# Banded attention followed by a leaky-ReLU MLP: an opening with sums ahead of products, the first hidden tiles of a half advanced pair by pair over four banks, and other gates for the loads of batches 1 and 2

## The chip, the core and the metric

The kernel runs on one core of one Trainium2 chip. The metric is the device time of one execution in microseconds, as the median over runs. The engines are named as in the profile: PE is TensorE's matmuls and PEld its weight loads, DVE is VectorE, ACT ScalarE, POOL GpSimd, SP SyncE (which here only issues DMAs). The letter q behind a name (SPq, ACTq) means the engine's instruction queue rather than its arithmetic.

## What is computed

Eight batches of eight heads attend over 576 tokens within a window of 32 to each side. The result, as 4608 tokens by 512 channels, goes through two matrices with a leaky ReLU between them.

```python
# q, k, v: (8, 8, 576, 64); w_in: (512, 2048); w_out: (2048, 512); all float32
scores = np.matmul(q, k.transpose(0, 1, 3, 2)) / np.sqrt(64)
mask = np.abs(pos[:, None] - pos[None, :]) <= 32
attn = softmax(np.where(mask, scores, -1e9))
x = np.matmul(attn, v).transpose(0, 2, 1, 3).reshape(4608, 512)
h = x @ w_in
out = np.maximum(0.01 * h, h) @ w_out
```

## The kernel before

**Units of work.** Two heads, p and p+4, share the 128 partitions and are called a pair. A half is 288 of a batch's 576 tokens. One attention step i is one pair of one half of one batch: `where(i)` (L233) gives batch i//8, half (i//4)%2 and pair i%4, so there are 64 steps. A half g of the MLP needs the four steps of that half, because `xT` (the attention output, transposed) holds one pair in each of its four 128-channel chunks.

**One batch on its way to a step.** SP loads q, k (`load_qk`, L64, two DMAs a pair) and v (`load_v`, L77, two DMAs a pair). `cast_qk` (L166) casts q and k to bf16, q on DVE or POOL and k on POOL. `transposes` (L190) turns them on PE into a bank of PSUM, ACT copies them to `qT` and `kT` (L208, L214), and `place_keys` (L220) lets DVE put the keys into the block-diagonal `kbd` (L226). `cast_v` (L172) puts v into the block-diagonal `vbd`. Both block-diagonal tiles must have been set to zero first, `clear` (L118) on ACT or a memset.

**One step.** `score` (L236) is five matmuls into `ps`, an exponential on ACT (`e`, L247) and the product with the band's mask on POOL (`pr`, L251). `weighted` (L267) multiplies `pr` by a block of ones for the row sums `s` (L275 and L278, or L273 after `join` has added the two parts of `pr`), then `pr` by v for `x` (five matmuls, L285); DVE takes the reciprocal `r` of `s` (L291) and multiplies `x` by it into `xT` (L293). `s` and `x` have one PSUM bank each (`xps`, L58), so the next `s` waits for this reciprocal and the next `x` for this multiplication.

**The MLP.** `h_tile(g, f)` (L299) is four accumulating matmuls, one for each pair's chunk c of `xT` (L304), and a leaky ReLU on ACT into `gT` (L308). There are 16 such tiles in a half. `o_tile(j)` (L312) is sixteen accumulating matmuls for 128 tokens (L321), a copy on ACT (L326) and a store that ACT issues (L327). Hidden tiles, output tiles and transposes rotate over the four banks of `mmps` (L56).

**The order.** `manual_schedule` (L45) keeps every engine in the order of the program text, so an instruction that waits holds back all that is behind it on its engine. Every DMA of SP and ACT takes the next of eight semaphores in turn, and its issue waits until the DMA that had that semaphore before it has landed, whichever queue issued that one. The opening (L424 to L485) is written out by hand: batch 0 is cast and transposed, steps 0 to 3 run one after another with `keep_busy` (L329: matmuls whose result nobody reads) between them, the weights are loaded by POOL (`load_w_in`, eight DMAs, L409; `load_w_out`, four, L415) between POOL's other work; then the 16 hidden tiles of half 0 with steps 4 to 7 between them, then batch 1's transposes between the 16 tiles of half 1, and scores 8 and 9. From L490 on a plan of matmul times sets for every step a due time, and `spend` (L512) calls `step` (L360) when the plan's clock passes it.

**Gates on the loads.** `load_qk(..., behind)` first copies one element of a given tile into the place that the load will fill (L70; `load_v`: L81). As the copy must follow the writer of that element, and the load must follow the copy, the load and all that SP issues later wait. Before, batch 1's q and k wait in this way for `w_in`'s second chunk of columns (L456), and batch 1's v for `w_out`'s second chunk (L470). Batch 2's q and k are issued with no gate, ahead of steps 8 to 11 (L521), and its v after steps 10 to 13 (L524).

Of the kernel before, what the change touches and what calls it, by code (L numbers as in the profile page):

```python
# [16 lines left out]
def kernel(  # L17
# [34 lines left out]
    prob = ctx.enter_context(tc.tile_pool(name="prob", bufs=4))  # L52
# [73 lines left out]
    clear(vbd[0], 1)  # L126

# [10 lines left out]
    for lo in (0, 64):  # L138
        w = win[lo:lo + 64]
        nc.gpsimd.affine_select(  # L140
            out=w, in_=w, compare_op=ALU.is_ge, fill=0.0,
            base=0, channel_multiplier=-1, pattern=[[0, 3], [1, 128]],
        )
        nc.gpsimd.affine_select(
            out=w, in_=w, compare_op=ALU.is_ge, fill=0.0,
            base=2 * W, channel_multiplier=1, pattern=[[0, 3], [-1, 128]],
        )
    win_f = win.rearrange("p n c -> p (n c)")
# [87 lines left out]
    def score(i):  # L236
        b, hf, p = where(i)
        ps = scps.tile([128, 1024], FP32, name="ps")
        c0 = 512 - HALF
        for blk, q0, n in WIN[hf]:  # L240
            nc.tensor.matmul(  # L241
                ps[:, c0:c0 + n], kbd[b % 2][:, p, blk],
                qT[b][:, p, q0:q0 + n], start=True, stop=True,
            )
            c0 += n
        e = attn.tile([128, NCOL], BF16, name="e")
        nc.scalar.activation(  # L247
            out=e, in_=ps[:, 512 - HALF:512 - HALF + NCOL], func=AF.Exp, scale=scale,
        )
        pr = prob.tile([128, NCOL], BF16, name="pr")  # L250
        nc.gpsimd.tensor_mul(pr, e, mask[hf])  # L251
        probs[i] = pr, None

    def join(i):
# [4 lines left out]
        both = prob.tile([128, HALF], BF16, name="both")  # L259
# [5 lines left out]
        probs[i] = pr, both  # L265

    def weighted(i):  # L267
        b, hf, p = where(i)
        pr, both = probs.pop(i)
        x = xps.tile([128, HALF], FP32, name="x")  # L270
# [3 lines left out]
        else:  # L274
# [6 lines left out]
            )  # L281
        c0 = 0
# [7 lines left out]
        r = attn.tile([128, HALF], FP32, name="r")  # L290
        nc.vector.reciprocal(r, s)  # L291
        t0 = (b * S + hf * HALF) % RING
        nc.vector.tensor_mul(xT[:, p, t0:t0 + HALF], x, r)  # L293
# [4 lines left out]

    def h_tile(g, f):  # L299

        t0 = g * HALF % RING
        h = mmps.tile([128, 512], FP32, name="mm", tag="mm")
        for c in range(DMC):
            nc.tensor.matmul(  # L304
                h[:, 0:HALF], w_in_bf[:, c, ts(f, 128)], xT[:, c, ds(t0, HALF)],
                start=(c == 0), stop=(c == DMC - 1),
            )
        nc.scalar.activation(  # L308
            out=gT[:, f, ds(t0, HALF)], in_=h[:, 0:HALF], func=AF.Prelu, alpha=0.01,
        )  # L310
# [49 lines left out]
    def step():  # L360
# [10 lines left out]
        if i < 7:  # L371
            score(i + 1)
        elif 8 <= i < NC - 2:
            nb, _, np_ = where(i + 2)
            if nb >= BY_DMA:
                step_transposes(8 * nb + 2 * np_ + 2)
                place_keys()
            score(i + 2)
# [28 lines left out]
    def load_w_in(f0, f1):  # L407
        for a in range(2):
# [20 lines left out]
    clear(vbd[0], 2)  # L429
    cast_v(0, 0)  # L430
    cast_qk(0, 2, nc.vector)
    score(0)
    load_w_in(0, 512)
    first_pair()
    clear(vbd[0], 3)
    cast_qk(0, 3, nc.vector)
    load_w_in(512, 1024)
    for i in range(NPAIR):
        score(i + 1)
        if i + 1 < NPAIR:  # L440
            cast_v(0, i + 1, on_act=True)
        if i < 2:
            load_w_in(1024 + 512 * i, 1536 + 512 * i)
        else:
            load_w_out(i - 2)
        if i > 0:
            keep_busy(3 if i == 1 else 2)
        weighted(i)
        if i == 0:
            first_pair()  # L450
    state["done"] = NPAIR

    for p in range(NPAIR):
        load_qk(1, p, w_in_bf[0:1, 0, 512:514] if p == 0 else None)  # L456
    keep_busy(2)
    step()
    load_w_out(2)
    load_w_out(3)  # L460
    for f in range(FFC):
        h_tile(0, f)
        if f in (2, 6, 10):
            step()
        if f % 4 == 3:
            nc.gpsimd.memset(kbd[1][:, f // 4], 0.0)
    cast_qk(1, 0, nc.vector)
    cast_qk(1, 1, nc.vector)
    for p in range(NPAIR):
        load_v(1, p, w_out_bf[0:1, 4, 0:2] if p == 0 else None)  # L470
    second = transposes(1)
    for f in range(FFC):
        h_tile(1, f)
        if f % 4 == 3:
            p = f // 4
            next(second)
            next(second)
            place_keys()
            if p + 2 < NPAIR:
                cast_qk(1, p + 2, nc.vector)  # L480
            nc.gpsimd.memset(vbd[1][:, p], 0.0)
        if f == 11:
            score(8)
    state["tp"] = 16
    score(9)  # L485
# [18 lines left out]
    due = []  # L504
    for i in range(8, NC):
        prev = 0.9 * O_US * 4 if i < 12 else at[i // 4 - 1] - LEAD
        due.append(prev + (at[i // 4] - LEAD + (1.2 if i < 12 else 0) - prev) * (i % 4 + 1) / 4)
# [4 lines left out]
    def spend(us):  # L512
        nonlocal clock, turn
        while due and due[0] <= clock:
            due.pop(0)
            i = state["done"]
            if i < 11:
                cast_v(1, i - 7)

            if i < 12:  # L520
                load_qk(2, i - 8)  # L521
            step()
            if 10 <= i < 14:
                load_v(2, i - 10)  # L524
# [42 lines left out]
```

## Time and profile before

| What | Value |
|---|---|
| three runs | 331.64 us median, 330.44 to 332.67 |
| profiled execution | 330.4 us, of which the profiled span is 328.7 us |
| busy share of the span | PE 94%, DVE 70%, ACT 66%, PEld 63%, POOL 55% |
| `h` matmuls, 128x288 (L304) | 1024, 286 ns each in the profile; sixteen in a row take 1.96 us |
| `o` matmuls, 128x512 (L321) | 592; sixteen in a row take 3.45 us |
| reciprocal (L291) | 64, 1954 ns each |
| multiplication into `xT` (L293) | 64, 458 ns each |
| loads | q and k 288 KB each, v 144 KB in each of two DMAs, `w_in` 256 KB and `w_out` 512 KB each as stored |

The span of 328.7 us lies inside the 330.4 us of the execution, so 1.7 us lie around it. A line of the timeline gives start, duration, engine, line of the program, operation, out<-in, number of instructions merged, and in brackets the idle time before it with what ended it. A line of the waits gives who waited for whom, the total in us, how often, and the longest. A matmul's own duration contains its passage through the array; what a row of matmuls costs is its end less its start.

### The profile page before, as it was taken

The page shows a single profiled execution, that of the slowest core. Times are in us where ns is not written, and L with a number is a line of the kernel's source. Part 1 is how long each engine was busy: PE and PEld are TensorE (multiplying, and loading weights), DVE is VectorE, ACT ScalarE, POOL GpSimd, SP SyncE. Part 2 cuts the span into 40 slices and gives each one's busy share as a digit, 9 for nine tenths or more (in the row PEclk, how much of TensorE's full clock was granted, in tenths as well). Part 3 has the DMA queues.
Part 4 walks back from the last instruction along what each step waited for, and adds up shares of the span by engine and source line. Part 5 has one row for each costly group of instructions (what it writes and reads, how often), then busy time and mean ns, then how long its engine had stood idle before and what let it go on. Part 6 is the DMA issues. An engine that isn't in the chain of part 4 may idle for free.

```text
span 328.7 us, 6685 instructions
## 1 busy us (share of the span) xinstructions
PE 308.3 (94%) x2533; PEld 207.3 (63%) x2533; DVE 228.5 (70%) x310; ACT 218.5 (66%) x432; POOL 180.3 (55%) x213
## 2 busy tenths in 40 slices
PE   2578999699999999999999999999999999999996
PEld 1446784367675676758485666767675767666653
DVE  4489744588795987879786988789768867565200
ACT  6775791358493674878988887878786655554541
POOL 7698747667783695519751497339642545221000
PEclk9999999999999999999999999999999999999999
DMA  8999979969995489935997199947831001010102
GB/s 181 215 199 220 269 179 208 235 164 231 200 212 162 152 146 208 226 106 125 194 232 146 64 160 226 194 127 94 173 90 65 34 3 63 2 64 3 64 8 89
DMA packets 80309, 47.11 MB, mean 143 GB/s; under 512 B 59156, under 2 KB 75796, under 8 KB 80276
## 3 DMA queue, kind: packets, MB, share of 16 engines
q1 hardware_dynamic: 70660, 33.04, 52.9%
q10 hardware_dynamic: 5328, 9.44, 8.4%
q0 software_dynamic: 4288, 4.20, 7.6%
q8 instruction: 20, 0.33, 0.4%
q14 instruction: 13, 0.11, 0.1%
HBM read 36.70 MB, written 9.44 MB: 140 GB/s over the span
## 4 chain that ended last, share of the span: by engine, by line
PE 79%; DMA 6%; DVE 6%; SPq 3%; ACT 3%; issue 1%; POOL 1%; ACTq 0%; DVEq 0%
PE mm L304 36%; PE mm L321 31%; DVE r L291 4%; PE x L285 4%; PE ps L241 4%; DMA kf<-in_k_dram 2%; DMA out_dram<-o_sb 2%; PE s L273 2%; SPq L83 2%; PE tp L200 2%; DMA vf<-in_v_dram 2%; ACT kT L214 1%; SPq L72 1%; DVE xT L293 1%; ACT qT L208 1%
## 5 line engine op out<-in xcount | busy, mean ns | idle before, releaser
L291 DVE RECIPROCAL r<-s 128x288 f32<-128x288 f32 x64 | 125.1, 1954 | 38.0 <-PE s L273 28.4
L251 POOL TENSOR_TENSOR pr<-e,mask 128x544 bf16<-128x544 bf16 x64 | 77.8, 1216 | 103.9 <-ACT e L247 82.1
L304 PE MATMUL mm<-xT,w_in_bf 128*128 128x288 bf16 x1024 | 133.5, 286 | 0.4 <-DVE xT L293 0.4
L321 PE MATMUL mm<-w_out_bf,gT 128*128 128x512 bf16 (+2 forms) x592 | 130.1, 373 | 0.0
L308 ACT ACTIVATE gT<-mm 128x288 bf16<-128x288 f32 x256 | 100.8, 415 | 20.6 <-PE mm L304 8.1
L304 PEld LDWEIGHTS <-w_in_bf 128*128 128x128 bf16 x1024 | 98.2, 98 | 24.7 <-issue 0.8
L321 PEld LDWEIGHTS <-gT 128*128 128x128 bf16 x592 | 56.4, 98 | 59.8
L247 ACT ACTIVATE e<-ps 128x544 bf16<-128x544 f32 x64 | 40.0, 624 | 26.2 <-DMA vf<-in_v_dram 4.8
L326 ACT ACTIVATE o_sb<-mm 128x512 f32<-128x512 f32 (+2 forms) x37 | 21.6, 585 | 53.7 <-PE mm L321 53.7
L226 DVE COPY kbd<-kT 64x576 bf16<-64x576 bf16 x64 | 28.5, 446 | 25.6 <-ACT kT L214 24.9
L178 POOL CAST vbd<-vf 64x576 bf16<-64x576 f32 x58 | 38.8, 669 | 2.0
L293 DVE TENSOR_TENSOR xT<-x,r 128x288 bf16<-128x288 f32 x64 | 29.3, 458 | 6.7
L168 POOL CAST kb<-kf 96x768 bf16<-96x768 f32 x32 | 27.5, 858 | 10.0 <-DMA kf<-in_k_dram 10.0
L241 PE MATMUL ps<-qT,kbd 128*128 128x128 bf16 (+2 forms) x320 | 26.8, 216 | 2.8 <-ACT e L247 2.8
L241 PEld LDWEIGHTS <-kbd 128*128 128x128 bf16 x320 | 20.8, 101 | 11.0 <-issue 3.3
L285 PE MATMUL x<-pr,vbd 128*128 128x128 bf16 (+2 forms) x320 | 26.3, 214 | 1.5 <-DVE xT L293 1.0
L262 DVE TENSOR_TENSOR both<-pr 128x256 bf16<-128x256 bf16 x52 | 23.4, 449 | 3.5 <-POOL pr L251 2.4
L285 PEld LDWEIGHTS <-vbd 128*128 128x128 bf16 x320 | 20.9, 99 | 5.0 <-issue 1.9
L264 DVE COPY both<-pr 128x32 bf16<-128x32 bf16 x52 | 23.8, 459 | 0.0
L168 POOL CAST qb<-qf 96x768 bf16<-96x768 f32 x24 | 19.7, 820 | 0.0
L208 ACT ACTIVATE qT<-qT 128x576 bf16<-128x576 bf16 x16 | 18.8, 1176 | 0.9 <-ACT o_sb L326 0.8
L214 ACT ACTIVATE kT<-kT 128x576 bf16<-128x576 bf16 x16 | 18.8, 1176 | 0.0
(39 smaller groups left out, 121.4 us busy)
## 6 DMA issues: line engine op xcount, KB each, us to landing
qf<-in_q_dram SPq DMA_DIRECT2D x32, 288.0 KB, 5.1
kf<-in_k_dram SPq DMA_DIRECT2D x32, 288.0 KB, 5.4
vf<-in_v_dram SPq DMA_DIRECT2D x64, 144.0 KB, 5.1
out_dram<-o_sb ACTq DMA_DIRECT2D x35, 256.0 KB, 2.5
w_in_bf<-in_moe_w_in_dram POOLq DMA_DIRECT2D x8, 256.0 KB, 6.7
w_out_bf<-in_moe_w_out_dram POOLq DMA_DIRECT2D x4, 512.0 KB, 13.0
qT<-qb SPq DMA_TRANSPOSE x16, 4.4
kT<-kb SPq DMA_TRANSPOSE x16, 4.2
```

The lines of the kernel that those rows point to most:

```text
L168: eng.tensor_copy(out=dst[:, p], in_=src[b, p].rearrange("p a (c d) -> p c a d", d=D),)
L178: nc.gpsimd.tensor_copy(out=vbd[b % 2][r, p, :, r], in_=vf[b, p][r])
L226: nc.vector.tensor_copy(out=kbd[b % 2][r, p, :, r], in_=kT[r].rearrange("p (n j) -> p n j", j=64),)
L241: nc.tensor.matmul(ps[:, c0:c0 + n], kbd[b % 2][:, p, blk], qT[b][:, p, q0:q0 + n], start=True, stop=True,)
L247: nc.scalar.activation(out=e, in_=ps[:, 512 - HALF:512 - HALF + NCOL], func=AF.Exp, scale=scale,)
L251: nc.gpsimd.tensor_mul(pr, e, mask[hf])
L285: nc.tensor.matmul(x[:, a:a + n], vbd[b % 2][:, p, blk, :], pr[:, c0:c0 + n], start=(n_ == 0), stop=(n_ == len(WIN[hf]) - 1), skip_group_c ...
L291: nc.vector.reciprocal(r, s)
L293: nc.vector.tensor_mul(xT[:, p, t0:t0 + HALF], x, r)
L304: nc.tensor.matmul(h[:, 0:HALF], w_in_bf[:, c, ts(f, 128)], xT[:, c, ds(t0, HALF)], start=(c == 0), stop=(c == DMC - 1),)
L308: nc.scalar.activation(out=gT[:, f, ds(t0, HALF)], in_=h[:, 0:HALF], func=AF.Prelu, alpha=0.01,)
L321: nc.tensor.matmul(o[:, lo:hi], gT[:, f, ds(128 * j % RING, 128)], w_out_bf[:, f, lo:hi], start=(f == 0), stop=(f == FFC - 1),)
```

## The change

- `weighted` is cut into `sums` (the sums' matmuls and the reciprocal), `product` (the five matmuls with v) and `scaled` (the multiplication into `xT`). Reciprocals get a pool of three buffers, `pr` six in place of four, the joined `pr` a pool of its own.
- The opening is written anew. Scores 0 and 1 come ahead of the third transposes, `sums(0)` between the two transposes of pair 2. All nine matmuls of `keep_busy` go. `w_in`'s first chunk is loaded in two parts, head group 0 after the second product with the mask and head group 1 after the third; the other `w_in` chunks follow, and `w_out`'s after the products with the mask of scores 4 and 5. ACT clears `vbd[0]` for pairs 0 to 2 at the start, POOL for pair 3.
- `h_first` computes the first four hidden tiles of a half chunk by chunk: the four matmuls for c = 0, one in each of four banks, then those for c = 1, and so on. In half 0, the products, sums and scores of pairs 2 and 3 stand ahead of c = 2 and c = 3.
- Batch 1's q, k and v are loaded in one run behind one gate, `w_out`'s first chunk. Batch 2's loads stand behind the steps: each pair behind its own step's `xT`.
- Batch 1's first two casts of q on DVE (`cast_qk(1, 0)`, `cast_qk(1, 1)`) stand ahead of the last step of half 1 (`second_half()` for i = 7), and `h_first(1)` follows that step. The transposes of batch 1's pair 0 come after tile 13 of half 1, those of pairs 1 to 3 and scores 8 and 9 among the output tiles, and steps 8 to 11 at fixed due times.

The order in which DVE has the instructions around that last step, as the changed program is compiled (its own line numbers: L287 the reciprocal, L172 the casts, L313 the multiplication, L230 the keys):

```
L287 Reciprocal r<-s
L172 TensorCopy qb<-qf   (batch 1, pair 0)
L172 TensorCopy qb<-qf   (batch 1, pair 1)
L313 TensorTensor xT<-x,r
L230 TensorCopy kbd<-kT
```

```diff
+    def sums(i):
         b, hf, p = where(i)
-        pr, both = probs.pop(i)
-        x = xps.tile([128, HALF], FP32, name="x")
+        pr, both, _ = probs[i]
         s = xps.tile([128, HALF], FP32, name="s")
         if both is not None:
             nc.tensor.matmul(s, ones_bd, both, start=True, stop=True)
...
+        r = recip.tile([128, HALF], FP32, name="r")
+        nc.vector.reciprocal(r, s)
+        probs[i][2] = r
+
+    def product(i):
+
+        b, hf, p = where(i)
+        pr = probs[i][0]
+        x = xps.tile([128, HALF], FP32, name="x")
         c0 = 0
         for n_, (blk, q0, n) in enumerate(WIN[hf]):
...
-        r = attn.tile([128, HALF], FP32, name="r")
-        nc.vector.reciprocal(r, s)
+        probs[i][1] = x
+
+    def place(i):
+
+        b, hf, p = where(i)
         t0 = (b * S + hf * HALF) % RING
-        nc.vector.tensor_mul(xT[:, p, t0:t0 + HALF], x, r)
+        return xT[:, p, t0:t0 + HALF]
+
+    def scaled(i):
+        _, x, r = probs.pop(i)
+        nc.vector.tensor_mul(place(i), x, r)
+
+    def weighted(i):
+        if probs[i][2] is None:
+            sums(i)
+        product(i)
+        scaled(i)
...
+    def h_first(g, hooks):
+
+        hs = [mmps.tile([128, 512], FP32, name="mm", tag="mm") for _ in range(4)]
         for c in range(DMC):
-            nc.tensor.matmul(
-                h[:, 0:HALF], w_in_bf[:, c, ts(f, 128)], xT[:, c, ds(t0, HALF)],
-                start=(c == 0), stop=(c == DMC - 1),
-            )
-        nc.scalar.activation(
-            out=gT[:, f, ds(t0, HALF)], in_=h[:, 0:HALF], func=AF.Prelu, alpha=0.01,
-        )
+            if c in hooks:
+                hooks[c]()
+            for f in range(4):
+                h_mms(g, f, hs[f], (c,))
+        for f in range(4):
+            h_out(g, f, hs[f])
...
-        if i < 7:
-            score(i + 1)
-        elif 8 <= i < NC - 2:
+        if 8 <= i < NC - 2:
...
-    def load_w_in(f0, f1):
-        for a in range(2):
+    def load_w_in(f0, f1, heads=(0, 1)):
+        for a in heads:
...
     cast_qk(0, 1, nc.vector)
     first_pair()
     first_pair()
-    clear(vbd[0], 2)
     cast_v(0, 0)
+    score(0)
     cast_qk(0, 2, nc.vector)
-    score(0)
-    load_w_in(0, 512)
-    first_pair()
-    clear(vbd[0], 3)
+    score(1)
+    load_w_in(0, 512, (0,))
+    next(first)
+    sums(0)
+    next(first)
+    product(0)
+    place_keys()
     cast_qk(0, 3, nc.vector)
+    scaled(0)
+    sums(1)
+    cast_v(0, 1, on_act=True)
+    score(2)
+    load_w_in(0, 512, (1,))
     load_w_in(512, 1024)
-    for i in range(NPAIR):
-        score(i + 1)
-        if i + 1 < NPAIR:
-            cast_v(0, i + 1, on_act=True)
-        if i < 2:
-            load_w_in(1024 + 512 * i, 1536 + 512 * i)
-        else:
-            load_w_out(i - 2)
-        if i > 0:
-            keep_busy(3 if i == 1 else 2)
+    next(first)
+    next(first)
+    place_keys()
+    product(1)
+    scaled(1)
+    cast_v(0, 2, on_act=True)
+    load_w_in(1024, 1536)
+    sums(2)
+    score(3)
+    load_w_in(1536, 2048)
+
+    def before_2():
+        product(2)
+        scaled(2)
+        cast_v(0, 3, on_act=True)
+        sums(3)
+        score(4)
+        load_w_out(0)
+
+    def before_3():
+        product(3)
+        scaled(3)
+        sums(4)
+        score(5)
+        load_w_out(1)
+
+    state["done"] = NPAIR
+
+    def second_half():
+
+        i = state["done"]
         weighted(i)
-        if i == 0:
-            first_pair()
-    state["done"] = NPAIR
-
-
-
-    for p in range(NPAIR):
-        load_qk(1, p, w_in_bf[0:1, 0, 512:514] if p == 0 else None)
-    keep_busy(2)
-    step()
+        if i < 7:
+            sums(i + 1)
+        if i < 6:
+            score(i + 2)
+        state["done"] += 1
+
+    h_first(0, {2: before_2, 3: before_3})
     load_w_out(2)
     load_w_out(3)
-    for f in range(FFC):
+
+    for p in range(NPAIR):
+        load_qk(1, p, w_out_bf[0:1, 0, 0:2] if p == 0 else None)
+    for p in range(NPAIR):
+        load_v(1, p)
+    second_half()
+    for f in range(4, FFC):
         h_tile(0, f)
-        if f in (2, 6, 10):
-            step()
-        if f % 4 == 3:
-            nc.gpsimd.memset(kbd[1][:, f // 4], 0.0)
+        if f in (7, 11):
+            second_half()
+        if f % 2 == 1:
+            nc.gpsimd.memset((kbd if f < 12 else vbd)[1][:, (f - 4) // 2 % 4], 0.0)
     cast_qk(1, 0, nc.vector)
     cast_qk(1, 1, nc.vector)
-    for p in range(NPAIR):
-        load_v(1, p, w_out_bf[0:1, 4, 0:2] if p == 0 else None)
     second = transposes(1)
-    for f in range(FFC):
+
+    def second_pair(p):
+        next(second)
+        next(second)
+        place_keys()
+        if p + 2 < NPAIR:
+            cast_qk(1, p + 2, nc.vector)
+
+    second_half()
+    h_first(1, {})
+    for f in range(4, FFC):
         h_tile(1, f)
-        if f % 4 == 3:
-            p = f // 4
-            next(second)
-            next(second)
-            place_keys()
-            if p + 2 < NPAIR:
-                cast_qk(1, p + 2, nc.vector)
-            nc.gpsimd.memset(vbd[1][:, p], 0.0)
-        if f == 11:
-            score(8)
+        if f == 13:
+            second_pair(0)
+        if f in (7, 9):
+            nc.gpsimd.memset(vbd[1][:, (f - 3) // 2], 0.0)
     state["tp"] = 16
-    score(9)
 
 
 
@@ -501,27 +574,35 @@
         if kind == "h" and f == 0:
             at[g] = t
         t += us
-    due = []
-    for i in range(8, NC):
-        prev = 0.9 * O_US * 4 if i < 12 else at[i // 4 - 1] - LEAD
-        due.append(prev + (at[i // 4] - LEAD + (1.2 if i < 12 else 0) - prev) * (i % 4 + 1) / 4)
+    due = [
+        (0.0, lambda: score(8)), (1.0, lambda: second_pair(1)), (2.6, lambda: second_pair(2)),
+        (3.2, lambda: score(9)), (4.4, lambda: second_pair(3)),
+    ]
+    due += [(6.0 + 1.9 * n, step) for n in range(NPAIR)]
+    for i in range(12, NC):
+        prev = at[i // 4 - 1] - LEAD if i >= 16 else 11.9
+        due.append((prev + (at[i // 4] - LEAD - prev) * (i % 4 + 1) / 4, step))
     clock = 0.0
     cast_v(1, 0)
     turn = 0
 
     def spend(us):
         nonlocal clock, turn
-        while due and due[0] <= clock:
-            due.pop(0)
+        while due and due[0][0] <= clock:
+            what = due.pop(0)[1]
+            if what is not step:
+                what()
+                continue
             i = state["done"]
             if i < 11:
                 cast_v(1, i - 7)
-
+            step()
+
+            mark = place(i)[0:1, 0:2]
             if i < 12:
-                load_qk(2, i - 8)
-            step()
+                load_qk(2, i - 8, mark)
             if 10 <= i < 14:
-                load_v(2, i - 10)
+                load_v(2, i - 10, mark)
 
```

## The prediction

> **What bounds the kernel now.** I read the page's slices first, then each engine's timeline for the first 70 us, then the waits. TensorE is busy nearly everywhere; its slices fall below 9 only in the first four and in the eighth (57.5 to 65.7 us). The DMA engines are full for the first 60 us.
>
> ```profile
> PE 308.3 (94%) x2533; PEld 207.3 (63%) x2533; DVE 228.5 (70%) x310; ACT 218.5 (66%) x432; POOL 180.3 (55%) x213
> ...
> PE   2578999699999999999999999999999999999996
> ...
> DMA  8999979969995489935997199947831001010102
> ```
>
> So a change of the opening is worth what it does to TensorE's time up to 70 us; from there both versions have the same work. Four rows of TensorE's timeline: from x of step 4 at 27.49 it runs without a gap through the 32 hidden tiles, and the first output matmul starts at 48.46.
>
> ```profile
> 27.49 0.40 PE L285 MATMUL x<-pr,vbd 128*128 128x64 bf16 x5 [0.15 <-DVE xT L293]
> 27.73 1.63 PE L304 MATMUL mm<-xT,w_in_bf 128*128 128x288 bf16 x12
> ...
> 48.46 5.34 PE L321 MATMUL mm<-w_out_bf,gT 128*128 128x512 bf16 x24
> ...
> 62.99 0.40 PE L241 MATMUL ps<-qT,kbd 128*128 128x64 bf16 x5 [2.16 <-ACT e L247]
> ```
>
> After that its rows show idle times of 0.34, 0.61, 2.16, 0.15 and 0.23, in all 3.5 us up to 70. The two longest end with `e` on ScalarE, which itself stood behind a store's issue that waited for batch 1's and batch 2's loads:
>
> ```profile
> PE ps L241 <- ACT e L247: 2.8, 2, 2.2
> ...
> ACT e L247 <- DMA vf<-in_v_dram: 4.8, 1, 4.8
> ...
> ACT e L247 <- DMA kf<-in_k_dram: 3.6, 1, 3.6
> ```
>
> VectorE's rows: the last step of half 1 is finished before batch 1's first casts, which wait for loads.
>
> ```profile
> 35.28 1.96 DVE L291 RECIPROCAL r<-s 128x288 f32<-128x288 f32 x1
> 37.34 0.46 DVE L293 TENSOR_TENSOR xT<-x,r 128x288 bf16<-128x288 f32 x1
> 37.71 1.49 DVE L168 CAST qb<-qf 96x768 bf16<-96x768 f32 x2
> ```
>
> SyncE's rows: a gate is issued when its writer has landed, and the loads behind it start when the gate's copy has landed: 4.5 us after its start the first time, 8.7 us the second.
>
> ```profile
> 22.95 0.73 SPq L70 DMA_DIRECT2D qf<-w_in_bf  x1
> ...
> 27.48 0.33 SPq L72 DMA_DIRECT2D qf<-in_q_dram  x1
> ...
> 28.39 0.40 SPq L72 DMA_DIRECT2D qf<-in_q_dram  x1
> ...
> 37.73 0.62 SPq L81 DMA_DIRECT2D vf<-w_out_bf  x1
> ...
> 46.42 6.38 SPq L83 DMA_DIRECT2D vf<-in_v_dram  x8
> ```
>
> **The opening up to half 1.** Score 0's `e` loses the clear ahead of it and starts at about 10.2 (11.22 before). From there by durations of the rows: `pr` 0 ends 12.1, sums 0 at 12.9 (low clock), reciprocal 0 at 14.9, pair 2's keys (0.91) 15.8, score 2 16.5, `e` 17.2, `pr` 2 18.4. Only then is the second part of `w_in`'s first chunk issued (14.78 before). The first q load, on an empty queue, landed in 3.4 us; the fastest of the eight `w_in` loads, all queued, in 5.9. So it lands between 21.8 and 24.3; batch 0's last load landed at 19.9, the queue is idle, so I take 22.2. The c = 0 and c = 1 matmuls wait for it ahead of x 2: eight at 0.24 (low clock) end 24.2, x 2 and its multiplication end 25.3 (24.98 before), reciprocal 3 and multiplication 3 end 27.7 (27.44 before). Sums ahead of products gained 2 us earlier, and the wait for `w_in` takes them back. Next, sums 5 wait for reciprocal 4 (28.2 to 30.15). From 30.2 TensorE has until c = 3 of half 1: twelve tiles (5.88), twelve matmuls (1.47) and eight small groups of 0.24: it gets there at 39.5, and reciprocal 7 ends about 38.2. The nine `keep_busy` matmuls lay in TensorE's waits for VectorE; taking them out saves nothing, and they count for the clock below.
>
> **The step that decides: multiplication 7.** In the changed order both batch-1 casts stand on VectorE between reciprocal 7 and multiplication 7. Behind it waits c = 3 of the first four hidden tiles of half 1, and behind those all of TensorE. The casts need the second q load, third in the run of batch 1, whose gate has moved from `w_in`'s second chunk to `w_out`'s first.
> - `w_out`'s first chunk landed at 32.9 (issued 24.07, 8.9 later) at the end of a stream without a hole: `w_in`'s eight loads land 1.32 apart. The later second load can open a hole of 0 to 2.6 us. I take 33.0.
> - The gate's copy: 4.5 or 8.7 by the rows above, 3.0 (a v load at 46.42 on idle engines) at the least. 8.7 was behind eight loads of its own queue, which is empty here, while `w_out`'s chunks 2 to 4 are moving as `w_in` was in the first case: 4.5, so 37.5.
> - First q issue to second q landed: 9.7 before (27.48 to 28.39 + 8.8) with `w_out` beside it all the time; 5.7 for batch 0 alone (0.81 to 1.74 + 4.8). A `w_out` chunk alone takes 2.6 (twice 1.32), so chunks 2 to 4 end at about 40.9: half the bandwidth is gone for 2.6 of the time. 5.7 + 1.3 = 7.0, so 44.5 (bounds 41.6 and 53.9).
> - Cast 0.56, multiplication 0.46, 0.15 to TensorE: c = 3 starts at 45.7, an idle time of 6.2 us where there was none.
>
> **What follows.** From c = 3 TensorE has 13 tiles less what is done (6.4), eight groups of transposes (2.04) and scores 8 and 9 (0.48), 8.9 us, to stand where it stood at 48.46. New gaps: score 8 follows pair 0's transposes after only two tiles. Before, transposes at 44.98 had keys placed at 47.69, 2.7 us; two groups and two tiles are 1.5; gap 1.2. Steps 8 to 11 come every 1.73 us of plan and 0.72 of their own, 2.45, against VectorE's 2.42: I allow 0.5, bounds 0 and 1.5. The stores no longer share semaphores with loads of batch 2, which now wait for their steps, so the 3.5 us go. Those loads land about 8 us after the `xT` of their step (4.5 and 3.4), four steps ahead of their casts: hidden by the steps of half 3, by 0 to 3 us.
>
> **The clock.** The page's clock row shows full speed throughout, but six transposes take 0.66 until 16.9 and 0.42 at 40: the rise lies at about 20.7 (two `keep_busy` matmuls: 0.63, the next two 0.59, three before them 1.49), 3.3 us after TensorE became dense at 17.4. Its last matmul ended at 325.7, and the windows show the clock falling at about 327.9, 2.2 us later:
>
> ```profile
> 327.00:328.00 1.00, 0.00 (x0) 0.00 (x0) 0.00 (x0) 0.00 (x0) 0.00 (x0) 0.96 0.22 64
> 328.00:328.70 0.70, 0.00 (x0) 0.00 (x0) 0.00 (x0) 0.00 (x0) 0.00 (x0) 0.50 0.00 0
> ```
>
> An idle time of 6.2 us is longer, so I expect the clock to fall and 3.3 us at half speed after it: 1.7 (0 if it holds, 6.4 if it stayed low through all hidden tiles).
>
> The Trainium skill ("TensorE: Matmul & The Clock Gate", Part 1) has the clock halved by default, raised after a busy window of about 3.4 us and lowered after an idle one, with windows that run freely. By it the loss would be 1.7 to 3.4 us, and the sum up to 1.7 higher. That rule speaks against this change twice: `keep_busy` goes and a long idle time comes. The fall after 2.2 us here is sooner than a whole such window after the last matmul.
>
> **Sum.** 45.7 + 8.9 + 1.2 + 0.5 + 1.7 = 58.0, against 48.5 + 3.5 = 52.0 before: 6.0 us later. On the profiled execution's 330.4 that gives 336.4. It lies 1.2 under the median of the three runs, 331.64, within their spread; I add nothing for that.
>
> No cost: clearing by ScalarE at the start (1.15, in its 1.32 idle ahead of the first `qT`) and by GpSimd (1.05, in 1.47 idle ahead of the first k cast), and the new pools. GpSimd's zeroing of the batch-1 tiles lies in its wait for k; without that cover it would be 1.05 each. The eight gate copies of batch 2 cost SyncE 0.6 to 0.7 each, with only loads behind them.
>
> **Rivals.**
> 1. The loads are in time (faster). If the second q load has landed by 38.2, c = 3 starts at 38.2 + 1.12 + 0.46 + 0.15 = 39.9, no clock is lost, and the sum is 50.5: 1.5 us sooner, 329; with an opening at full clock, 1.6 sooner again. I put it at 328. For it: VectorE would have the casts behind it. Against: batch 0, `w_in` and a `w_out` chunk had the engines full up to 32.9. Break-even is a landing at 40.1.
> 2. A short stall (within 1%). Gate 3.0 and loads 5.7 after 33.0: 41.7, c = 3 at 42.9; the clock holds: 53.5, or 332. For it: `w_out`'s chunks 2 to 4 may be issued too late to stand in the gate's way. Against: in my chain they are issued from 30.6.
> 3. A long stall (slower still). Gate 8.7 and loads 9.7: landing 51.4, c = 3 at 52.6, the sum 64.9: 343.
>
> **How the numbers follow.** My forecast 0.70 (333.5 to 340), rival 1 0.05, rival 2 0.17, rival 3 0.08. About 1% (3.3 us) is what a measurement of this kernel can tell from no change. Rival 2 and 0.03 of mine lie within it: same 0.20, faster 0.05, slower 0.75. The range leaves out rival 1, the very short stalls and most of rival 3: 331.5 to 341.
>
> **What would show it.** In the changed profile: VectorE's casts of q waiting for a q load and standing between reciprocal and multiplication; TensorE idle for about 6 us ahead of an `h` matmul, ended by `xT`, at 39 to 46; slower matmuls after it; about 1 us idle ahead of score 8; no long wait of `e` for loads at 55 to 66. I am wrong if `w_out`'s first chunk or the gate lands much sooner than 33 and 37.5, or if TensorE has no gap there.

## The result and the profile after

| | before | after |
|---|---|---|
| median | 331.43 us (330.44 to 332.67, four runs) | 353.90 us (352.49 to 355.16, four runs) |
| profiled execution, its span | 330.4 us, 328.7 us | 355.2 us, 353.5 us |
| ratio of after to before | | 1.0675 [1.062, 1.073] |

The change costs 22.5 us in the medians and 24.8 us in the two profiled spans; the forecast was 6.0 us (the profiled execution of before is the fastest of its four, that of after the slowest, hence the difference of the two). The page of after, in the rows that answer to those shown of before, with the row of the granted clock:

```profile
PE 313.5 (89%) x2503; PEld 210.6 (60%) x2524; DVE 229.5 (65%) x310; ACT 218.9 (62%) x431; POOL 181.4 (51%) x214
...
PE   2557929999893699999999999999999999999996
...
PEclk9998967999998599999999999999999999999999
DMA  8999999036377984997299926993682101010102
```

A slice is now 8.84 us. TensorE has two holes, in the sixth slice (44 to 53 us, digit 2) and in the 13th and 14th (106 to 124 us, digits 3 and 6), and the granted clock dips at both. I had forecast only the first. How much each is worth is read from VectorE's reciprocals, of which both kernels have 64 in the same order of steps: the 17th stands at 104.29 us in after and at 90.38 in before, 13.9 us later; the 18th at 120.14 and 95.39, 24.75 later; the last at 328.52 and 303.83, 24.7 later. The 17th and 18th, in after and then in before:

```profile
104.29 1.96 DVE L287 RECIPROCAL r<-s 128x288 f32<-128x288 f32 x1 [1.56 <-PE s L277]
...
120.14 1.94 DVE L287 RECIPROCAL r<-s 128x288 f32<-128x288 f32 x1
```

```profile
90.38 1.96 DVE L291 RECIPROCAL r<-s 128x288 f32<-128x288 f32 x1 [1.25 <-PE s L273]
...
95.39 1.96 DVE L291 RECIPROCAL r<-s 128x288 f32<-128x288 f32 x1 [0.55 <-PE s L273]
```

So 13.9 us are lost in the opening and by the few steps behind it, 10.8 us within one step, and from there on nothing.

**The first hole.** TensorE in after (start, duration, engine, line, operation, count, idle time before it):

```profile
25.04 2.08 PE L327 MATMUL mm<-xT,w_in_bf 128*128 128x288 bf16 x8 [3.77 <-DMA w_in_bf<-in_moe_w_in_dram]
...
34.07 3.43 PE L327 MATMUL mm<-xT,w_in_bf 128*128 128x288 bf16 x16
...
42.70 1.69 PE L327 MATMUL mm<-xT,w_in_bf 128*128 128x288 bf16 x12
51.33 8.41 PE L327 MATMUL mm<-xT,w_in_bf 128*128 128x288 bf16 x44 [6.94 <-DVE xT L313]
...
62.33 0.41 PE L245 MATMUL ps<-qT,kbd 128*128 128x96 bf16 x5 [1.11 <-DVE kbd L230]
62.58 1.89 PE L363 MATMUL mm<-w_out_bf,gT 128*128 128x512 bf16 x7
```

The idle time of 6.94 us ahead of c = 3 is the one that the prediction named. VectorE and SyncE at that place:

```profile
40.81 1.95 DVE L287 RECIPROCAL r<-s 128x288 f32<-128x288 f32 x1
47.87 0.56 DVE L172 CAST qb<-qf 96x768 bf16<-96x768 f32 x1 [5.11 <-DMA qf<-in_q_dram]
50.35 0.56 DVE L172 CAST qb<-qf 96x768 bf16<-96x768 f32 x1 [1.93 <-DMA qf<-in_q_dram]
50.83 0.45 DVE L313 TENSOR_TENSOR xT<-x,r 128x288 bf16<-128x288 f32 x1
```

```profile
37.60 0.73 SPq L72 DMA_DIRECT2D qf<-w_out_bf  x1
42.14 0.34 SPq L74 DMA_DIRECT2D qf<-in_q_dram  x1
```

Reciprocal 7 is done at 42.76, its multiplication starts at 50.83, and what stands between are the two casts and their waits for q. The gate's copy goes out when `w_out`'s first chunk has landed, and q is issued 4.54 us after it. The windows around the hole (us, busy time of PE, PEld, DVE, ACT and POOL with counts, granted clock, share and GB/s of the DMA engines):

```profile
47.00:51.00 4.00, 0.00 (x0) 0.00 (x0) 1.21 (x3) 0.00 (x0) 0.82 (x1) 0.50 1.09 232
51.00:57.00 6.00, 5.67 (x24) 3.49 (x24) 0.27 (x1) 2.96 (x8) 3.59 (x4) 0.50 1.25 194
57.50:59.50 2.00, 2.00 (x19) 1.61 (x17) 0.00 (x0) 1.64 (x5) 1.33 (x2) 1.00 1.17 195
```

The clock was halved while TensorE waited and stayed so for about 6 us of work.

**The second hole.** TensorE and then GpSimd in after:

```profile
109.10 0.40 PE L298 MATMUL x<-pr,vbd 128*128 128x96 bf16 x5
118.27 0.66 PE L204 MATMUL tp<-ident,qb 96*128 96x96 bf16 x6 [8.77 <-POOL qb L172]
118.73 4.24 PE L327 MATMUL mm<-xT,w_in_bf 128*128 128x288 bf16 x20
```

```profile
106.46 0.66 POOL L182 CAST vbd<-vf 64x576 bf16<-64x576 f32 x1 [4.02 <-DMA vf<-in_v_dram]
107.28 0.67 POOL L182 CAST vbd<-vf 64x576 bf16<-64x576 f32 x1 [0.16 <-DMA vf<-in_v_dram]
114.69 1.47 POOL L182 CAST vbd<-vf 64x576 bf16<-64x576 f32 x2 [6.74 <-DMA vf<-in_v_dram]
116.24 1.21 POOL L255 TENSOR_TENSOR pr<-e,mask 128x544 bf16<-128x544 bf16 x1
117.39 0.82 POOL L172 CAST qb<-qf 96x768 bf16<-96x768 f32 x1
```

TensorE's row names the cast of q, but that cast is only what came last. Follow GpSimd back: the cast of q stands behind a product with the mask, that behind two casts of batch 2's v, and those wait 6.74 us for a load. The loads themselves, in SyncE's rows:

```profile
99.00 0.64 SPq L83 DMA_DIRECT2D vf<-xT  x1
102.94 1.61 SPq L85 DMA_DIRECT2D vf<-in_v_dram  x2
...
106.79 0.66 SPq L83 DMA_DIRECT2D vf<-xT  x1
111.38 1.31 SPq L85 DMA_DIRECT2D vf<-in_v_dram  x2
```

From a gate's issue to that of the load behind it the queue is kept for 3.9 and 4.6 us, and the next gate is issued behind the loads that were let go (with loads of batch 3 between). The eight gates of batch 2 together keep it for 24.0 us (1.6, 3.0, 3.2, 2.4, 2.2, 3.2, 3.9 and 4.6, read in the same way). It is the copies that keep it, not the `xT` that they read: only the first two gates were issued as their `xT` was written (74.28 and 76.93), the last one at 106.79, 15.9 us after its own was done (90.88). SyncE's waits from 84 to 118 us say the same of the v loads:

```profile
SPq L85 <- DMA vf<-xT: 11.5, 4, 3.9
```

In before GpSimd has six of these casts in a row without a wait:

```profile
87.43 4.31 POOL L178 CAST vbd<-vf 64x576 bf16<-64x576 f32 x6
```

### The profile page after: what moved, and what is told of

The parts are those of the page before. It is cut to its first block, busy times and chain, and to the rows that moved or that the text cites. A ratio compares the mean times of both kernels' runs of the same rounds, so it can differ in the third digit from the quotient of the medians.

```text
span 353.5 us, 6671 instructions
## 1 busy us (share of the span) xinstructions
PE 313.5 (89%) x2503; PEld 210.6 (60%) x2524; DVE 229.5 (65%) x310; ACT 218.9 (62%) x431; POOL 181.4 (51%) x214
## 4 chain that ended last, share of the span: by engine, by line
PE 67%; DMA 11%; DVE 6%; issue 5%; POOL 4%; ACT 3%; SPq 2%; ACTq 0%; DVEq 0%; POOLq 0%
PE mm L327 29%; PE mm L363 28%; PE ps L245 4%; PE x L298 3%; DMA qf<-in_q_dram 3%; DMA kf<-in_k_dram 3%; DVE r L287 3%; POOL pr L255 2%; PE tp L204 2%; DMA out_dram<-o_sb 2%; DMA w_in_bf<-in_moe_w_in_dram 1%; PE s L277 1%; DVE kbd L230 1%; DMA vf<-xT 1%; DMA qf<-w_out_bf 1%
## 5 line engine op out<-in xcount | busy, mean ns | idle before, releaser
L327 PE MATMUL mm<-xT,w_in_bf 128*128 128x288 bf16 x1024 | 141.2, 295 | 11.6 <-DVE xT L313 7.8
L287 DVE RECIPROCAL r<-s 128x288 f32<-128x288 f32 x64 | 125.0, 1954 | 32.8 <-PE s L277 30.4
L327 PEld LDWEIGHTS <-w_in_bf 128*128 128x128 bf16 x1024 | 101.5, 101 | 40.4 <-issue 12.5
L230 DVE COPY kbd<-kT 64x576 bf16<-64x576 bf16 x64 | 28.4, 444 | 32.5 <-ACT kT L218 32.0
L313 DVE TENSOR_TENSOR xT<-x,r 128x288 bf16<-128x288 f32 x64 | 29.3, 458 | 13.0 <-PE x L298 7.0
L172 POOL CAST kb<-kf 96x768 bf16<-96x768 f32 x32 | 27.7, 865 | 8.4 <-DMA kf<-in_k_dram 8.4
L204 PE MATMUL tp<-ident,qb 96*128 96x96 bf16 x96 | 7.9, 228 | 16.3 <-POOL qb L172 8.8
L172 POOL CAST qb<-qf 96x768 bf16<-96x768 f32 x24 | 19.7, 820 | 0.0
```

Of the source, the lines that this page charges most:

```text
L172: eng.tensor_copy(out=dst[:, p], in_=src[b, p].rearrange("p a (c d) -> p c a d", d=D),)
L230: nc.vector.tensor_copy(out=kbd[b % 2][r, p, :, r], in_=kT[r].rearrange("p (n j) -> p n j", j=64),)
L313: nc.vector.tensor_mul(place(i), x, r)
L327: nc.tensor.matmul(h[:, 0:HALF], w_in_bf[:, c, ts(f, 128)], xT[:, c, ds(g * HALF % RING, HALF)], start=(c == 0), stop=(c == DMC - 1),)
```

## The experiments

The theory from the two traces (A): two separate costs, one from the casts of q ahead of multiplication 7, one from the gates on batch 2's loads. Against it: that the clock, not the waits, makes the difference; that the removed `keep_busy` does; that the gates only cost together with the new opening. Ratios are to the kernel before, run beside each of these on the same chip (medians of 330.63 to 330.69 us); after was measured beside a median of 331.43, so a difference from after in the medians is uncertain by that 0.8 us besides the intervals. Line numbers are those of each kernel.

**The casts put behind the last step of half 1.**

```diff
-    cast_qk(1, 0, nc.vector)
-    cast_qk(1, 1, nc.vector)
     second = transposes(1)
...
     second_half()
+    cast_qk(1, 0, nc.vector)
+    cast_qk(1, 1, nc.vector)
     h_first(1, {})
```

> The changed kernel with the two casts of batch 1's q put behind multiplication 7 instead of ahead of it; nothing else. Theory A (two stalls: multiplication 7 behind casts that wait for a gated load, 6.9 us and the low clock after it, 2.9 us; and later batch 2's loads behind a chain of gates): c = 3 of half 1 starts at about 44 instead of 51.3, batch 1's keys then wait 1 to 3 us for their loads, the second idle time at about 110 stays near 9 us; 345 to 347 us. Rival B (the new opening without keep_busy costs the time, and what follows only waits for loads that are late anyway): the same wait comes back at batch 1's first transposes, 351 to 354.

Measured 346.52 us, 1.0485 [1.0429, 1.054]: 7.4 us less than after. TensorE no longer waits for `xT` there; smaller waits come up behind it (1.00 us for `kbd`, 1.81 for the cast of k), and the second hole stays, 8.97 us. So the first hole is the casts' place, and it is worth less than its length and its clock together (6.9 + 2.6, below), since the late loads are waited for elsewhere.

**Batch 2's loads without gates.**

```diff
-                load_qk(2, i - 8, mark)
+                load_qk(2, i - 8)
...
-                load_v(2, i - 10, mark)
+                load_v(2, i - 10)
```

> The changed kernel without the one-element copies ahead of batch 2's loads; the loads are still issued after their steps. Theory A: the 8.8 us that TensorE waits for transposes at about 110 to 118 go, with the 1.9 us of low clock after them; 343 to 346, a store or two on ScalarE held up by the loads included. Rival C (that wait comes from the new due times and from steps that come too early for their loads, not from the gates): the wait stays above 5 us, 350 to 354.

Measured 342.21 us, 1.0347 [1.0314, 1.0381]: 11.7 us less than after. The second hole is gone; the same twenty `h` matmuls that took 4.24 us behind it follow without a wait:

```profile
107.34 0.40 PE L298 MATMUL x<-pr,vbd 128*128 128x96 bf16 x5
107.58 0.42 PE L204 MATMUL tp<-ident,qb 96*128 96x96 bf16 x6
107.84 2.62 PE L327 MATMUL mm<-xT,w_in_bf 128*128 128x288 bf16 x20
```

By these rows the hole's price is 8.77 us of waiting, 4.24 - 2.62 = 1.62 of slower `h` matmuls and 0.66 - 0.42 = 0.24 of slower transposes: 10.6 us, against the 10.8 of the reciprocals. The first hole stays (7.65 us).

**Both at once.**

> Both edits: casts behind multiplication 7, no gates on batch 2's loads. Theory A: the two gains add, 334 to 338, still 3 to 6 us over the kernel before for the later opening (TensorE reached the first output matmul at 62.6 in the changed kernel; 52 to 54 here). Rival B: 342 to 346.

Measured 334.55 us, 1.0102 [1.0064, 1.014]. Against after that is 19.4 us less, and 7.4 + 11.7 = 19.1: the two costs add. (Each taken against the before beside it, the three are 18.6, 6.6 and 11.0 us, so they add to within about 1 us.) 3.9 us are left. The rows show waits of TensorE that come to more than that: 3.33 us for `w_in`'s second part, 0.65, 1.34 and 0.67 for products with the mask, 0.98 and 1.70 for casts of k, 0.77 for `kbd`; before has waits of its own, 3.5 us of them ahead of half 2, and how the two sets leave 3.9 was not worked out.

**Batch 1's gate back on `w_in`'s second chunk, the casts still ahead.**

```diff
-        load_qk(1, p, w_out_bf[0:1, 0, 0:2] if p == 0 else None)
+        load_qk(1, p, w_in_bf[0:1, 0, 512:514] if p == 0 else None)
```

> The changed kernel with the gate of batch 1's loads put back to w_in's second chunk, where it was in the kernel before; casts still ahead of multiplication 7, batch 2's gates kept. Theory A (the cast order costs nothing by itself, it only hands the loads' lateness to the hidden tiles): the second q load lands at 40 to 43 instead of 50.3, the wait ahead of c = 3 shrinks from 6.9 to under 2 us; 344 to 347. A rival that the cast order itself is the cost: the wait stays at 5 us or more, 351 to 354.

Measured 350.20 us, 1.0569 [1.0505, 1.0632]: the direction was right, the size was not. The copy landed 4.5 us after its issue (26.13 to 30.58), 11.6 us sooner than in after. VectorE and then GpSimd:

```profile
38.76 1.95 DVE L287 RECIPROCAL r<-s 128x288 f32<-128x288 f32 x1
40.62 4.52 DVE L172 CAST qb<-qf 96x768 bf16<-96x768 f32 x2
45.06 0.44 DVE L313 TENSOR_TENSOR xT<-x,r 128x288 bf16<-128x288 f32 x1
```

```profile
41.09 2.06 POOL L538 MEMSET vbd<- 128x1152 bf16 x2
43.10 2.72 POOL L172 CAST kb<-kf 96x768 bf16<-96x768 f32 x2
```

The hole is 3.23 us in place of 6.94, and it is another hole: neither cast has idle time ahead of it, so they no longer wait for q. They run long, 2.94 and 1.66 us where each took 0.56 in after, while GpSimd zeroes tiles and casts k beside them. That is 3.5 us more than in after, as much as the whole hole. So the place of the casts makes the hole in both; the gate made its length in after, and here the casts' own length does.

**`w_in`'s two parts issued together**, on top of both mended:

```diff
-    load_w_in(0, 512, (0,))
+    load_w_in(0, 512)
...
-    load_w_in(0, 512, (1,))
```

> The run with both edits (casts behind multiplication 7, no gates on batch 2's loads) and, in addition, both parts of w_in's first chunk issued at the first place, ahead of the third product with the mask. Theory A: TensorE's wait for w_in ahead of c = 0 (3.3 us there) falls to about 1 us, since the second part is issued near 15.3 instead of 19.4 and lands near 22; all that follows comes about 2 us sooner, 331.5 to 333.5 us. Rival (the opening is held by VectorE's reciprocals, w_in's wait only covers them): no change, 334 to 335.

Measured 333.52 us, 1.0089 [1.0054, 1.0124]. The wait for `w_in` falls from 3.33 to 0.79 us, but the time cannot be told from that of the kernel without it (1.0102 [1.0064, 1.014]). The gain that the rows show is not established in the time.

**The kernel before with batch 2's gates.** This tells whether the gates cost by themselves. The loads of q and k also move behind their step, as in the change; two runs have that move without the gates, the one above without batch 2's gates, which has no second hole, and the one below with v let go early, which costs nothing.

```diff
-            if i < 12:
-                load_qk(2, i - 8)
             step()
+            pb, ph, pp = where(i)
+            t0 = (pb * S + ph * HALF) % RING
+            mark = xT[0:1, pp, t0:t0 + 2]
+            if i < 12:
+                load_qk(2, i - 8, mark)
             if 10 <= i < 14:
-                load_v(2, i - 10)
+                load_v(2, i - 10, mark)
```

> The kernel before with one part of the change alone: batch 2's loads are issued behind their steps and behind a one-element copy of that step's xT. Theory A (the gates form a chain on SyncE, 1.6 to 4.6 us for each of eight copies, and the last v load of batch 2 comes too late for its cast): TensorE gets a wait of 5 to 9 us ahead of a transpose near 100 us, and a low clock after it; 336 to 343. Rival C (they only hurt in the changed kernel, whose steps 8 to 11 come later against the plan): 329 to 332.

Measured 340.32 us, 1.0289 [1.026, 1.0317]: 9.7 us more than before, with the old opening. The same hole at the same operation:

```profile
103.46 0.66 PE L200 MATMUL tp<-ident,qb 96*128 96x96 bf16 x6 [10.01 <-POOL qb L168]
```

So the gates need nothing of the new opening to cost.

**Only the gates on v taken away**, in after (`load_v(2, i - 10, mark)` becomes `load_v(2, i - 10)`).

> The changed kernel with the four copies ahead of batch 2's v loads taken out and the four ahead of its q and k kept. Theory A (the chain is long because each copy holds all of SyncE's queue for its step and its 1.6 to 4.6 us; the last v load and the q load of batch 3 behind it are what come too late): the wait at 110 to 118 falls from 8.8 to between 0 and 3 us, 342 to 347. If q and k's gates alone made the chain too long, the wait stays above 6 us, 351 to 354.

Measured 348.94 us, 1.0545 [1.0511, 1.058], a miss: of the second hole half is left.

```profile
110.80 0.66 PE L204 MATMUL tp<-ident,qb 96*128 96x96 bf16 x6 [4.38 <-POOL qb L172]
```

I had put all of it on the v gates. What keeps the last v load late in this run is in SyncE's waits for 84 to 112 us: a q load of batch 3, ahead of that v load in the queue, waits for the semaphore of an output store.

```profile
SPq L74 <- DMA out_dram<-o_sb: 7.5, 1, 7.5
```

In the run above that has none of the eight gates there is no second hole. That the q and k gates push the queue into this store's way fits, but no run took them away alone.

**The kernel before without its nine `keep_busy` matmuls** (both places deleted).

> The kernel before without its nine idle-filling matmuls. Theory A (they buy only the clock): TensorE's clock rises later, after it has become dense with the hidden tiles at about 27.7, so at 31 to 34 instead of 20.7, and 3 to 6 us run at half speed: 332 to 334. Rival B (the opening's clock is a large part of the loss): 336 or more. No effect: 330 to 331.

Measured 330.71 us, 1.0011 [0.9991, 1.0032], a miss: no cost. Transposes and matmuls run at their slow durations up to about 32 us instead of 20.7, so the opening does fall behind; but of the 3.5 us that TensorE idles in before ahead of half 2, 1.08 are left, in two waits at 69.4 and 70.0 us (0.80 and 0.28), and half 2 begins at 70.22, where it began at 70.06. The later TensorE arrives, the shorter it waits for the loads there. Putting `keep_busy` back into after was not tried.

**The first hole filled with matmuls nobody reads**, in after, to price the clock:

```diff
+    def fill():
+        s = xps.tile([128, HALF], FP32, name="s")
+        for _ in range(54):
+            nc.tensor.matmul(s, ones_bd, mask[0][:, 0:HALF], start=True, stop=True)
+
-    h_first(1, {})
+    h_first(1, {3: fill})
```

> The changed kernel with 54 added matmuls of 288 columns, whose result nobody reads, between c = 2 and c = 3 of the first hidden tiles of half 1, where TensorE waits 6.9 us; at full clock they last 6.6 us. Theory A (the stall also costs the clock: TensorE ran at half speed from 51.3 to 57.2, worth 2.9 us): the stall's end stays where it is, the clock stays up, and the time falls by 2 to 3.5 us, 350.5 to 352. If the clock cost nothing, the time stays at 353 to 355 or grows by what the filling overlaps.

Measured 352.26 us, 1.0645 [1.0616, 1.0674]. TensorE's rows:

```profile
42.82 6.78 PE L554 MATMUL s<-mask,ones_bd 128*128 128x288 bf16 x54
50.32 5.84 PE L327 MATMUL mm<-xT,w_in_bf 128*128 128x288 bf16 x44 [0.71 <-DVE xT L313]
```

The same 44 matmuls take 5.84 us where they took 8.41, so the clock's part of the first hole is 2.6 us in the rows. In the medians it is 1.6 us (0.9 against the before beside each), and the intervals of the two kernels overlap, so the sign is not settled by the time alone. The waiting stays, c = 3 starts at 50.32 where it started at 51.33: the clock is the smaller part.

**The kernel before with v let go early and batch 2's q and k behind their step** (no gate on batch 1's v; `load_qk(2, i - 8)` moved below `step()`). This was to win before's 3.5 us of idle time.

> The kernel before with batch 1's v loads in one run behind q and k, without their own gate, and batch 2's q and k issued after their step instead of ahead of it, without gates. Theory A: v lands at about 54 instead of 57, the stores' issues on ScalarE wait less for the loads that share their semaphores, and of the 3.5 us that TensorE idles between 54 and 70 in the kernel before 1.5 to 3 go: 327.5 to 329.5. If the stores' waits come from batch 2's loads instead, little changes: 330 to 331.

Measured 330.46 us, 0.9994 [0.998, 1.0008], a miss: no gain. The wait for v's load is gone, and the next one takes its place, now for batch 2's q:

```profile
62.17 0.62 ACT L247 ACTIVATE e<-ps 128x544 bf16<-128x544 f32 x1 [3.38 <-DMA qf<-in_q_dram]
```

**The changed opening mended in all of this at once**: late casts, no gates on batch 2, `w_in`'s parts together, the rest of the weights each one product with the mask later, batch 1's gate on `w_in`'s second chunk, pair 0's transposes two tiles sooner.

```diff
-    load_w_in(0, 512, (0,))
+    load_w_in(0, 512)
...
-    load_w_in(0, 512, (1,))
...
-        load_qk(1, p, w_out_bf[0:1, 0, 0:2] if p == 0 else None)
+        load_qk(1, p, w_in_bf[0:1, 0, 512:514] if p == 0 else None)
...
-        if f == 13:
+        if f == 11:
             second_pair(0)
```

> The changed kernel mended at five places: casts behind multiplication 7, no gates on batch 2's loads, w_in's first chunk issued in one go, the other w_in and w_out chunks one at a time between the products with the mask, batch 1's gate on w_in's second chunk, and the transposes of batch 1's pair 0 two tiles sooner. Theory A (what is left of the loss is GpSimd issuing five loads ahead of a product with the mask, 2.7 us of waits on TensorE, and batch 1's k coming late, 2.2 us): 328 to 331, level with the kernel before or a little under. Rival (the order of the opening itself loses): 332 or more.

Measured 338.32 us, 1.022 [1.0195, 1.0245], a clear miss, slower than the two mends alone. TensorE reaches the output tiles at 48.47 us, as early as before, and then stands:

```profile
53.05 1.02 PE L363 MATMUL mm<-w_out_bf,gT 128*128 128x512 bf16 x4 [1.31 <-DMA w_out_bf<-in_moe_w_out_dram]
...
60.84 0.45 PE L204 MATMUL tp<-ident,kb 96*128 96x96 bf16 x6 [4.03 <-ACT qT L212]
```

```profile
59.72 0.38 ACTq L369 DMA_DIRECT2D out_dram<-o_sb  x1
60.14 0.65 ACT L212 ACTIVATE qT<-tp 128x576 bf16<-128x576 bf16 x1 [5.43 <-DMA qf<-in_q_dram]
```

`w_out` now moves at the same time as batch 1's loads and lands later, and the first store's issue holds ScalarE for a load of q. The last `w_out` chunk lands at 53.0 here and at 46.1 with the two mends alone. That batch 1's loads, let go sooner, take from `w_out` and the stores more than they win fits these rows; with all of these edits in one run, which of them costs is not shown.

**The kernel before with its first four stores issued by SyncE.** The same wait of ScalarE, in a store's issue, holds up the kernel before at 52 to 63 us.

```diff
-            nc.scalar.dma_start(out=out[ts(j, 128), lo:hi], in_=o_sb[:, lo:hi])
+            (nc.sync if j < 4 else nc.scalar).dma_start(out=out[ts(j, 128), lo:hi], in_=o_sb[:, lo:hi])
```

> The kernel before with the stores of the first four output tiles issued by SyncE instead of ScalarE. Theory A (of the 3.5 us that TensorE idles between 54 and 70 in the kernel before, 2.8 are ScalarE held up by a store's issue that waits for a load on the same semaphore): those waits go, 327.5 to 329. If the loads that now stand behind the stores on SyncE come late for their casts, it is 330 or more.

Measured 327.78 us (327.31 to 328.65), 0.9908 [0.9885, 0.993]: just under 1% faster than before, and so faster than both kernels. From the first output matmul to the first `h` matmul of half 2 TensorE has one idle time, 0.15 us, where before has 3.5 us:

```profile
50.13 5.34 PE L321 MATMUL mm<-w_out_bf,gT 128*128 128x512 bf16 x24
...
61.85 0.40 PE L285 MATMUL x<-pr,vbd 128*128 128x96 bf16 x5 [0.15 <-DVE xT L293]
...
67.74 2.49 PE L304 MATMUL mm<-xT,w_in_bf 128*128 128x288 bf16 x19
```

```profile
54.40 0.38 SPq L327 DMA_DIRECT2D out_dram<-o_sb  x1
```

The first store is issued as soon as its copy is done (at 54.38, by ScalarE's rows), where before it was issued at 57.08, 4.4 us after its copy, and `e` behind it. The store's wait for a load is gone rather than moved, and the semaphores recorded in the two traces show why. In before the store takes its turn behind seven loads of batch 2 and gets the semaphore of the last of batch 1's v loads, issued at 52.00. Here it takes its turn right behind batch 1's v loads and gets the semaphore of the first of them, issued at 46.11 and landed at 49.2. So it is the store's place in the turn that gained the time, and the engine that issues it only in that it set this place.

## Why the prediction was wrong

The forecast was right in direction and in the first mechanism, and wrong in size: 6.0 us, where the spans show 24.8. Point by point:

1. **The step that failed: batch 2's loads, "hidden by the steps of half 3, by 0 to 3 us", and their eight gate copies, "0.6 to 0.7 each, with only loads behind them".** I priced one load behind its step. The eight gates are in one queue, in order. Each keeps the queue until its copy has landed (24.0 us for the eight), and the next pair's gate, the v loads and batch 3's loads stand behind it; the steps' `xT` held up only the first two. The delays add up over the queue until the last v load is issued at 111.38. Behind that load stands GpSimd with a cast, behind the cast a product with the mask and the next batch's casts, and behind those TensorE. Cost: 10.8 us by the reciprocals, 11.7 by the run without the gates (11.0 against the before beside it), 9.7 in the kernel before. That the gates cause it was shown by runs both ways; the split between v's gates and those of q and k was not settled.
2. **"The step that decides: multiplication 7": right mechanism, late by 5.6 us.** Forecast 45.7, measured 51.33. The idle time is near the forecast (6.94 against 6.2), because TensorE itself came late too (44.4 = 51.33 - 6.94 in place of 39.5). The mis-sized term is `w_out`'s first chunk, which I let land at 33.0 as before while the program issues it only after score 4's product with the mask (29.28 to 30.49 us): issued 30.44, landed 37.5. I had worked out that chain for `w_in`, and for `w_out` only beside the sum, where chunks 2 to 4 are issued from 30.6. The copy's 4.5 us was exact; the second q landed at 50.3, 8.2 us after its run began, where I took 7.0.
3. **"The opening up to half 1": late by 2.7 us at c = 1.** I took 22.2 for `w_in`'s second part. GpSimd issued it at 19.62 (forecast 18.4) and it landed at 24.9. The matmuls ended at 26.9 in place of 24.2. Then came short waits for products with the mask (0.65 and 1.33 us), and a stretch at half clock from 33.3 to 36.7 us, in which sixteen `h` matmuls took 3.43 us instead of 2.12. The last two were not in the forecast.
4. **"The clock": 1.7 forecast, 2.6 measured** at the first hole (8.41 - 5.84), within the bounds of 0 and 6.4 given for it. The estimate that the prediction made from the window of about 3.4 us in the Trainium skill ("TensorE: Matmul & The Clock Gate", Part 1), 1.7 to 3.4, holds the 2.6 as well. At the second hole it was 1.9, and the run that filled the first hole shows that the price goes when the idle time is filled.
5. **"What follows": right but for about 1 us.** The gap ahead of score 8 was 1.11 us against 1.2, and the long waits of `e` for loads at 55 to 66 us did go. At the first output matmul TensorE is 62.58 - 48.46 = 14.1 us behind before, with six groups of transposes and a score still to do that before had done (six times 0.26 and 0.25, 1.8 us): 15.9. At half 3's first `h` matmul, where both have done the same work, it is 102.23 - 88.33 = 13.9. So 2.0 us came back: the 3.5 of before's idle time, less three new waits of 0.98, 0.40 and 0.17 us for `kbd` and `xT`. Of these 1.55 us the forecast had allowed 0.5, for steps 8 to 11 (where the 0.40 came).
6. **"Taking them out saves nothing", of `keep_busy`: right in the kernel before** (1.0011), and the cost in clock that I let count for them was hidden by a later wait.

The sum: 6.0 forecast, 5.6 from c = 3's late start, 0.9 from the clock (2.6 against 1.7) and 1.05 from the three waits beyond the 0.5 allowed make 13.55, against 13.9 measured ahead of the second hole; the gates' 10.8 make it 24.35, of 24.8 between the spans. The rest, 0.4, I cannot place. Of the rivals, the third came near the landing (51.4 against 50.3), by a copy of 8.7 us that didn't happen, and none had a second hole. By the terms of the prediction the break-even landing in the first is 40.2, not 40.1, which changes nothing.

## What to carry to other kernels

A gate moves a wait into an in-order queue, so price it by the queue: the landing time of every gate in series, then all loads behind the last one, then whoever casts them and what that engine has behind the cast. When a load's gate is moved, work out anew when that gate's writer is itself issued, by the program's new order, and do not carry its landing time over. An instruction that can only wait, such as a store's issue or a cast of the next batch, belongs behind the current step's last instruction or on an engine with nothing urgent behind it; here issuing four stores from SyncE in place of ScalarE, which also moved their turn for a semaphore ahead of seven loads, gave 2.9 us of 330.7.

## What the runs showed of the hardware that was not expected

- A gate's copy of one element keeps its queue for 1.6 us at the least and 4.6 at the most in after, and 8.7 in before behind eight loads of its own queue. The copies are all of one size, so the size says nothing of the cost of the gate.
- The granted clock comes back late: halved during the first hole, it came back 5.9 us after matmuls resumed (51.33 to 57.2), and at the second hole after 3.8 us (118.27 to 122.05). It also fell once behind short waits: in after five matmuls of a score took 0.40 us at 30.77 and 0.66 at 33.61, with nothing between that idled longer than 1.33 us, while a wait of 2.16 us in before changed nothing. In the run without batch 2's gates the same place has two waits of 1.33 and 1.34 us, and the sixteen `h` matmuls behind them took 2.12 us, so the clock stayed up there; what decides is open.
- VectorE's cast of q takes 0.56 us while GpSimd is idle (47.87 and 50.35 in after). Beside GpSimd's zeroing of a tile it took 2.94 us (40.62, with the gate back on `w_in`) and 2.04 (52.37, with late casts). The rows show the two together; no run took GpSimd's work away to prove it.
- Slower matmuls in an opening can cost nothing at all: some 11 us more at the low clock (up to about 32 in place of 20.7) left the time at 1.0011 [0.9991, 1.0032], because TensorE then reached a wait for loads that it would have had anyway.
